# First two units of an RWKV-6 and SiLU kernel: values of the first queries in array quarters, a key turn moved behind the products for x, values reversed by VectorE

## Chip, cores and metric

The kernel runs on one core of one Trainium2 chip. The metric is the device time of one execution in microseconds (us). Three runs of the kernel before gave 600.97, 601.18 and 601.67 us, so its median is 601.18.

## What is computed

The reference is an attention block of the RWKV-6 kind (4 batches, 8 heads, 768 tokens, 48 channels a head), whose output becomes x of a two-layer block with a SiLU between the layers. All data are float32.

```python
for t in range(S):
    cur = np.einsum('bhd,bhe->bhde', u[None] * kt, vt)
    y[:, :, t] = np.einsum('bhd,bhde->bhe', rt, state + cur)
    state = wt[:, :, :, None] * state + np.einsum('bhd,bhe->bhde', kt, vt)
x = y.transpose(0, 2, 1, 3).reshape(3072, 384)
h = x @ w_in                                   # 384 x 2048
out = (h * (1.0 / (1.0 + np.exp(-h)))) @ w_out # 2048 x 384
```

## The kernel before

**Units.** The recurrence is cut into chunks of 128 tokens. A unit is one chunk of two batches (NB = 2, called b below); there are 12 units. Within a chunk the output is a masked product: scores of queries against keys, then scores times values, plus what the state of earlier chunks gives. Queries and keys of the heads lie in pairs: head 2p is on partitions 0 to 47 and head 2p + 1 on 64 to 111 (e = 0 and 1). Scores are built in seven levels (`scores(i, l)`): level l is the part of the triangle in which query and key are in sibling blocks of 2^l tokens. TensorE makes the products of a level into PSUM (L704, L712), and VectorE copies the part that the level's mask keeps into `score` (`keep_masked`, L722); some parts are copied by ScalarE (L741). Between levels the keys and queries are multiplied by products of w: `grow_keys` on GpSimd (L645), `grow_queries` on VectorE (L627), `odd_keys` on ScalarE (L615), `product` on GpSimd (L422), `start_keys` (L669), `odd_ones` (L659). The diagonal with u is a sum over channels (`bonus`, `bonus_sum`), spread by a small matmul (`bonus_spread`, L590) and written into `score` by VectorE (`bonus_write`, L604).

**The second batch stands in reverse.** For b = 1 keys, scores and values are kept with the tokens of the chunk in reverse order. In `score` the partition is the key. For the first 64 queries only the keys of the first 64 tokens count: partitions 0 to 63 for b = 0, and 64 to 127 for b = 1; the other half of those columns of `score` holds zeros. The values of b = 1 therefore have to be reversed as well: `reverse_v` (L410). In units 0 and 1 their load (`load_values`, L138) brings the 128 tokens in order, TensorE multiplies them by a mirrored identity (L414), and ScalarE copies the product back (L415). From unit 2 on the load comes in four DMAs of 32 tokens, the four groups in reverse order (L143), and one VectorE `stream_shuffle` reverses the 32 partitions within each group (L417).

**Outputs of a unit.** In units 0 and 1 there is no earlier state. `y(i, b)` (L873) makes scores times values: for each pair p and each e one matmul of 128 keys by 64 columns (48 channels and 16 that are overwritten or not used), over 128 queries (L879), into one PSUM bank per b; ScalarE copies it out to `yt` (L883). `dense_x(i, b)` then makes x from `yt` with twelve records of 128x128 matmuls (L917) and ScalarE, in one case VectorE, copies it into `xt` (L919). `turn_apart(i)` (L814) turns the grown keys back to token rows with 16 transposes (L820), `turn_k` copies them out (L828), and `update(i, b)` makes from them and the values the new state (L893; copied by L909). From unit 2 on, `y_state` and `y_values` do the work of `y`; they already take the first 64 queries of half of the heads with 64 keys alone (L851), and the rest with 128 keys (L865).

**The layers.** `up(i, m)` makes 256 hidden columns of a unit's 256 tokens (L1001), and ScalarE applies SiLU (L1010). `down` (L1023) and, later, `quarter` (L1067) make the output.

**Weights are rounded on the way.** In the first 100 us the 16 pieces of the weights are loaded (`load_weight`, L206) and each is rounded by a chain over three engines: ScalarE's `tail_weight` (L231, into the PSUM tile p_w) and `head_weight` (L223, L225), VectorE's `join_weight` (L242, L243, which first needs that ScalarE part and frees p_w at its end), GpSimd's `add_weight` (L255). A later piece is loaded into the place that a joined one has left. The diagonal of unit 0 also sits in p_w until L604 has read it.

**Order.** The order is written by hand: the steps stand in lists that `do` calls one after the other, and each engine takes its own instructions in that order. The first two units are written out step by step (L1108 to L1164), the others by `mix`. All loads in this part go through SP's queue, each issue also waiting for the landing of the issue eight places before it. The part around the change is, from the end of unit 0's scores:

```python
do((bonus, 1, 0), (bonus, 1, 1), (bonus, 1, 2), *both(y, 0), (turn_apart, 0), (join_weight, 0), (add_weight,),
   (product, 1, 0), (tail_weight, 1), (turn, 1, 0, "k"), (join_weight, 1), (dense_x, 0, 0), (turn, 1, 1, "k"),
   (dense_x, 0, 1), (grow_queries, 1, 0), (odd_ones, 1), (tail_weight, 2), (turn_k, 0), (head_weight, 2),
```

PSUM tiles p_m and p_sc are two banks each, taken by turns by `bank`; p_h has two buffers. `y(0, b)` uses p_h, `y(1, b)` uses p_m.

Of the kernel before, what the change touches and what calls it, by code (L numbers as in the profile page):

```python
# [8 lines left out]
F32 = mybir.dt.float32  # L9
# [29 lines left out]
def kernel(  # L39
# [11 lines left out]
    nc = tc.nc  # L51

    B, H, S, D = r.shape
    DM, DF = moe_w_in.shape
    L = 128
    NL = 7
    NB = 2
    NP = H // 2
    PD = 64
# [8 lines left out]
    NTOK = 2  # L68
# [8 lines left out]
    ps = ctx.enter_context(tc.tile_pool(name="ps", bufs=1, space=bass.MemoryType.PSUM))  # L77
# [6 lines left out]
    def bank(name, *dims):  # L84

        have = banks[name][turns_of[name] % 2][:]
        turns_of[name] += 1
        steps, n = [], 1
        for d in dims[::-1]:
            steps.insert(0, [n, d])  # L90
            n *= d
        return bass.AP(tensor=have.tensor, offset=have.offset, ap=[have.ap[0], *steps])
# [4 lines left out]
    vt, vq, whole = {}, {}, {}  # L97
# [28 lines left out]
    def load_values(i):  # L126
        n, b0 = units[i]
        t0 = n * L

        rooms = [pin.tile([128, H * D + PD - D], F32, name=name, bufs=2) for name in ("vt", "vq")]  # L130
        if n == 0:
            for room in rooms:
                nc.vector.memset(room[:, H * D:], 0.0)
        whole[i] = rooms
        vt[i], vq[i] = (room[:, 0:H * D].rearrange("p (h d) -> p h d", h=H) for room in rooms)
        nc.sync.dma_start(out=vt[i], in_=v[b0, :, t0:t0 + L, :].rearrange("h t d -> t h d"))
        if i < NTOK:
            nc.sync.dma_start(out=vq[i], in_=v[b0 + 1, :, t0:t0 + L, :].rearrange("h t d -> t h d"))  # L138
            return

        for g in range(4):
            t1 = t0 + L - (g + 1) * 32
            nc.sync.dma_start(out=vq[i][g * 32:(g + 1) * 32], in_=v[b0 + 1, :, t1:t1 + 32, :].rearrange("h t d -> t h d"))  # L143
# [134 lines left out]
    load_tokens(1)  # L278
    load_weight(1)
    load_values(0)  # L280
    for i in due[-1][2:]:
        load_weight(i)
    load_values(1)

    ident = const.tile([128, 128], F32, name="ident")
# [47 lines left out]
    NSC = 1  # L333
    score = const.tile([128, NSC, 2, Q, L], F32, name="score")
# [74 lines left out]

    def reverse_v(i):  # L410
        flat = vq[i].rearrange("p h d -> p (h d)")
        if i < NTOK:
            p_v = bank("p_m", H * D)
            nc.tensor.matmul(p_v, lhsT=mirror, rhs=flat, start=True, stop=True)  # L414
            nc.scalar.copy(out=flat, in_=p_v)  # L415
            return
        nc.vector.stream_shuffle(out=flat, in_=flat, mask=list(range(31, -1, -1)))  # L417
# [53 lines left out]
    at = 768  # L471
# [358 lines left out]
    p_yt, p_kv, yt = {}, {}, {}  # L830
# [28 lines left out]
    def y_values(i, e):  # L859
# [9 lines left out]
        for x in range(2):  # L869
            nc.scalar.copy(out=yt[i][PD * e:PD * e + D, x::2, :, :],  # L870
                           in_=p_yt[i, e][PD * x:PD * x + D].rearrange("p (q b) t -> p q b t", b=NB))

    def y(i, b):  # L873

        p_yt[i, b] = ps.tile([128, NP, L], F32, name="p_h", bufs=2) if i == 0 else bank("p_m", NP, L)
        for p in range(NP):
            for e in range(2):
                h = 2 * p + e
                nc.tensor.matmul(p_yt[i, b][PD * e:PD * e + PD, p, :], lhsT=whole[i][b][:, h * D:h * D + PD],  # L879
                                 rhs=score[:, i % NSC, e, b * NP + p, :], start=(p == 0), stop=(p == NP - 1))  # L880
        if b == 0:
            yt[i] = pt.tile([128, NP, NB, L], F32, name="yt", bufs=1)
        nc.scalar.copy(out=yt[i][:, :, b, :], in_=p_yt[i, b])  # L883
# [49 lines left out]
    def both(fn, i, *args):  # L933
        return [(fn, i, b, *args) for b in range(NB)]
# [159 lines left out]
    def do(*steps):  # L1094
        for fn, *args in steps:
            fn(*args)
# [20 lines left out]
    for l in range(1, NL):  # L1117
        do((scores, 0, l), *[(grow_keys, 0, l + 1)] * (l + 1 < NL), *others[l])

    do((bonus, 1, 0), (bonus, 1, 1), (bonus, 1, 2), *both(y, 0), (turn_apart, 0), (join_weight, 0), (add_weight,),  # L1120
       (product, 1, 0), (tail_weight, 1), (turn, 1, 0, "k"), (join_weight, 1), (dense_x, 0, 0), (turn, 1, 1, "k"),
       (dense_x, 0, 1), (grow_queries, 1, 0), (odd_ones, 1), (tail_weight, 2), (turn_k, 0), (head_weight, 2),
       (start_keys, 1, nc.gpsimd, True), (add_weight,), (up, 0, 0), (join_weight, 2), *blocks[4:8],
       (start_keys, 1, nc.gpsimd, False), (add_weight,), (tail_weight, 3), (odd_keys, 1, 1), (head_weight, 3), (grow_keys, 1, 1),
       (scores, 1, 1, (join_weight, 3)), (add_weight,), (up, 0, 1), (tail_weight, 4), (grow_keys, 1, 2), (head_weight, 4),
# [1 line left out]


    others = {1: [(bonus_sum, 1, 0), (bonus_sum, 1, 1), (load_rk, 2), *blocks[8:12]], 2: [*both(update, 0)],
              3: [(bonus_spread, 1), (reverse_v, 1), (clear, 1), (load_values, 2)]}  # L1130

    def piece(i):

# [2 lines left out]
    for m in range(1, 4):  # L1136
        do((piece, m + 3), (scores, 1, m + 1), (grow_keys, 1, m + 2), (up, 0, m + 2), *others[m])
    do((head_weight, 8), (join_weight, 7), (scores, 1, 5), (grow_keys, 1, 6), (add_weight,), (tail_weight, 8), (up, 0, 6),
       (bonus_write, 1))

    do((scores, 1, NL - 1), (bonus, 2, 0), (bonus, 2, 1), (join_weight, 8), (add_weight,), (bonus_sum, 2, 0), (bonus, 2, 2), (up, 0, 7), *both(y, 1), (turn_apart, 1),
       (tail_weight, 9), (turn_k, 1), (dense_x, 1, 0), (head_weight, 9, [0]), (dense_x, 1, 1), (head_weight, 9, [1]),
       (join_weight, 9), (add_weight,), (tail_weight, 10), (head_weight, 10), *both(update, 1), (bonus_sum, 2, 1), (load_rk, 3), (up, 1, 0), *both(turn, 2, "w"))
    blocks = block_loads(3)
# [64 lines left out]
```

## Time and profile before

| | us |
|---|---|
| median of three runs | 601.18 |
| the profiled execution | 601.21 |
| its span in the profile | 599.4 |
| TensorE busy (matmuls) | 591.4 |
| VectorE busy | 415.2 |
| GpSimd busy | 363.6 |
| ScalarE busy | 232.8 |

Times in the profile count from the start of the span. PE is TensorE, PEld its weight loads, DVE VectorE, ACT ScalarE, POOL GpSimd and SP the queue that issues loads. A float32 matmul is recorded as two records, so "x32" on L879 is 16 matmuls. A busy TensorE isn't TensorE at its peak, since matmuls overlap and their ends are modelled. Instructions of ScalarE, VectorE and GpSimd overlap their neighbours by up to about 0.1 us, so starts are the better measure. The granted clock of TensorE is 1.0 over the whole span.

The stretches that the change touches: unit 0's y at 29.4 to 32, its x at 32.5 to 36, unit 1's `reverse_v` at 58.8 to 60.3, unit 1's y at 66.7 to 68.6, and its x at 69.2 to 72.2. Busy times there, from the table of windows:

| window | PE | DVE | ACT | POOL |
|---|---|---|---|---|
| 26 to 36 | 9.37 | 8.17 | 6.89 | 8.59 |
| 36 to 46 | 9.24 | 7.90 | 9.69 | 10.00 |
| 46 to 56 | 9.49 | 9.69 | 9.01 | 7.89 |
| 56 to 64 | 7.91 | 7.73 | 7.18 | 7.55 |
| 64 to 76 | 12.00 | 8.82 | 9.69 | 8.17 |
| 76 to 90 | 13.60 | 11.53 | 11.70 | 10.97 |

### The profile page before, as it was taken

To read this page: it belongs to the slowest core of one execution; us is meant where nothing else is said; L and a number is where in the kernel's file an instruction comes from. 1 tells how busy PE (TensorE), PEld (TensorE's weight loads), DVE (VectorE), ACT (ScalarE), POOL (GpSimd) and SP (SyncE) were. 2 spreads that over 40 slices of the span, in tenths; PEclk is the share of its full clock that TensorE was granted. 3 is DMA by queue.
4 is the path that set the end of the run, shared out by engine and by line. 5 is a ranking of instruction groups with operands and counts; after the bars stand their busy time and mean duration, and the time that the engine had idled before them with its cause. 6 is when DMAs were issued, how large, how long until landed. Compare 5 with 4: busy or idle time off the path is not lost.

```text
span 599.4 us, 15477 instructions
## 1 busy us (share of the span) xinstructions
PE 591.4 (99%) x6142; PEld 529.8 (88%) x6142; DVE 415.2 (69%) x709; ACT 232.8 (39%) x516; POOL 363.6 (61%) x414
## 2 busy tenths in 40 slices
PE   8999999999999999999999999999999999999997
PEld 8787876799899899899889889889889889889997
DVE  7879788798696695696695696686587587551041
ACT  6788884431530530540440351361351242240110
POOL 6998778357678668278478478478478558500000
PEclk9999999999999999999999999999999999999999
DMA  9966793343542543642642643643553531101000
GB/s 227 299 145 165 161 298 47 58 77 48 128 61 59 108 65 56 136 61 52 137 61 52 137 65 54 131 61 53 118 76 53 115 55 27 37 2 27 27 1 26
DMA packets 203080, 53.45 MB, mean 89 GB/s; under 512 B 186752, under 2 KB 194816, under 8 KB 203008
## 3 DMA queue, kind: packets, MB, share of 16 engines
q1 hardware_dynamic: 201424, 51.88, 42.1%
q8 instruction: 48, 0.79, 0.5%
q10 hardware_dynamic: 1584, 0.59, 0.5%
q14 instruction: 24, 0.20, 0.1%
HBM read 43.21 MB, written 5.24 MB: 81 GB/s over the span
## 4 chain that ended last, share of the span: by engine, by line
PE 87%; POOL 5%; DVE 4%; ACT 3%; issue 1%; POOLq 0%; DVEq 0%; ACTq 0%
PE p_h L1001 38%; PE p_o L1067 33%; PE p_m L1023 3%; PE p_sc L704 3%; PE p_m L865 2%; PE p_m L844 2%; PE p_m L704 2%; POOL w_in_sb L255 1%; POOL tk L645 1%; PE p_sc L893 1%; POOL w_out_sb L255 1%; DVE score L722 1%; PE p_m L820 1%; POOL tw L422 1%; DVE p_w L242 1%
## 5 line engine op out<-in xcount | busy, mean ns | idle before, releaser
L1001 PE MATMUL p_h<-xt,w_in_sb 128*128 128x256 f32 x1152 | 258.9, 382 | 0.8 <-POOL tk L669 0.7
L1001 PEld LDWEIGHTS p_h<-xt,w_in_sb 128*128 128x128 f32 x1152 | 215.9, 190 | 31.8 <-POOL tk L669 0.9
L1010 ACT ACTIVATE gt<-p_h 128x512 f32<-128x512 f32 x90 | 53.5, 596 | 181.5 <-PE p_h L1001 181.2
L645 POOL TENSOR_TENSOR tk<-tk,tw 128x256 f32<-128x256 f32 x128 | 94.5, 760 | 35.1 <-issue 21.0
L1067 PE MATMUL p_o<-own,temps 128*128 128x192 f32 x528 | 88.1, 326 | 0.1
L1067 PE MATMUL p_o<-w_out_sb,gt 128*128 128x192 f32 x508 | 87.4, 328 | 0.0
L1067 PEld LDWEIGHTS p_o<-own,temps 128*128 128x128 f32 x528 | 86.0, 190 | 0.5 <-DVE temps L1076 0.4
L507 POOL TENSOR_TENSOR ruk<-tokens_rk 128x768 f32<-128x768 f32 (+1 forms) x32 | 51.0, 1606 | 55.8 <-DMA tokens_rk<-in_k_dram 40.2
L1067 PEld LDWEIGHTS p_o<-w_out_sb,gt 128*128 128x128 f32 x508 | 82.7, 190 | 0.6
L1049 DVE TENSOR_TENSOR temps<-gt 128x256 f32<-128x256 f32 x84 | 57.8, 688 | 22.4 <-ACT gt L1010 22.4
L422 POOL TENSOR_TENSOR tw<-tw 128x256 f32<-128x256 f32 (+6 forms) x83 | 43.5, 524 | 35.8 <-DVE tw L374 31.9
L627 DVE TENSOR_TENSOR tr<-tr,tw 128x512 f32<-128x512 f32 x61 | 52.6, 862 | 18.0 <-PE p_m L704 14.3
L615 ACT COPY tk<-tk 128x256 f32<-128x256 f32 x52 | 21.0, 403 | 101.6 <-POOL tk L645 68.2
L722 DVE COPY_PREDICATED score<-mask,p_sc 128x512 f32<-128x512 int8 x42 | 31.2, 798 | 3.5 <-PE p_sc L704 3.3
L1049 DVE TENSOR_TENSOR temps<-temps,gt 128x256 f32<-128x256 f32 x43 | 32.3, 752 | 1.5
L1076 DVE TENSOR_TENSOR temps<-p_o,partial 128x192 f32<-128x192 f32 x22 | 7.9, 357 | 34.0 <-PE p_o L1067 24.8
L1076 DVE TENSOR_TENSOR partial<-p_o,partial 128x192 f32<-128x192 f32 x33 | 11.7, 356 | 28.2 <-PE p_o L1067 28.2
L1067 PE MATMUL p_o<-w_out_sb,temps 128*128 128x192 f32 x176 | 30.4, 326 | 0.0
L870 ACT COPY yt<-p_m 48x512 f32<-48x512 f32 x40 | 23.2, 580 | 15.7 <-PE p_m L865 11.9
L541 DVE TENSOR_REDUCE block_sums<-ruk 128x4 f32<-128x192 f32 (+1 forms) x48 | 24.2, 546 | 7.1 <-POOL ruk L507 7.1
L1067 PEld LDWEIGHTS p_o<-w_out_sb,temps 128*128 128x128 f32 x176 | 28.9, 190 | 0.0
L898 POOL TENSOR_TENSOR state<-state,tw 128x512 f32<-128x512 f32 x16 | 21.9, 1386 | 10.3 <-PE p_m L844 10.3
(191 smaller groups left out, 816.8 us busy)
## 6 DMA issues: line engine op xcount, KB each, us to landing
w_out_sb<-in_moe_w_in_dram SPq DMA_DIRECT2D x6, 768.0 KB, 7.7
w_out_sb<-in_moe_w_out_dram SPq DMA_DIRECT2D x4, 768.0 KB, 5.7
own<-in_moe_w_out_dram SPq DMA_DIRECT2D x4, 768.0 KB, 6.0
tokens_rk<-in_r_dram SPq DMA_DIRECT2D x8, 384.0 KB, 4.3
tokens_rk<-in_k_dram SPq DMA_DIRECT2D x8, 384.0 KB, 5.3
tokens_w<-in_w_dram SPq DMA_DIRECT2D x8, 384.0 KB, 6.5
xt<-yt SPq DMA_DIRECT2D x60, 48.0 KB, 1.9
raw<-in_w_dram SPq DMA_DIRECT2D x80, 32.0 KB, 2.0
```

The lines of the kernel that those rows point to most:

```text
L422: engine.tensor_tensor(out=up, in0=t[:, :, 0::2], in1=t[:, :, 1::2], op=ALU.mult)
L507: mul = lambda out, one, two: nc.gpsimd.tensor_tensor(out=out, in0=one, in1=two, op=ALU.mult)
L541: add = lambda out, have: nc.vector.tensor_reduce(out=out, in_=have, axis=mybir.AxisListType.X, op=ALU.add)
L627: nc.vector.tensor_tensor(out=odd, in0=odd, in1=tw[i][l][:, :, 0::2][:, :, :, None].to_broadcast([128, Q, L >> (l + 1), c]), op=ALU.mult)
L645: nc.gpsimd.tensor_tensor(out=out, in0=have, in1=odd_products(i, l, b, *blocks), op=ALU.mult)
L704: nc.tensor.matmul(to, lhsT=tk[i][rows, X[l % 2] + p, x * m:(x + 1) * m], rhs=have, start=True, stop=True)
L722: nc.vector.copy_predicated(out=dst, mask=masks[l][:, :, None].to_broadcast([128, NB, NP, ni, c]), data=sc[e].rearrange("p (b q) (i c) -> ...
L870: nc.scalar.copy(out=yt[i][PD * e:PD * e + D, x::2, :, :], in_=p_yt[i, e][PD * x:PD * x + D].rearrange("p (q b) t -> p q b t", b=NB))
L1001: nc.tensor.matmul(p_h[:, a, :], lhsT=w_in_sb[:, c, f * 128:(f + 1) * 128], rhs=xt[i][:, c, :], start=(c == 0), stop=(c == KC - 1))
L1010: nc.scalar.activation(out=gt[i, m], in_=p_h, func=AF.Silu)
L1049: nc.vector.tensor_tensor(out=out, in0=one, in1=two, op=op)
L1067: nc.tensor.matmul(p, lhsT=left(f), rhs=right[:, f, :], start=(f == 0), stop=(f == FH - 1))
```

## The change

It has three parts, all in units 0 and 1.

- y in quarters: a new step `y_first(i)` takes the first 64 queries of all heads and both b. For each p, e and b it is one matmul of 64 keys (the half that counts) by 64 columns over 64 queries, so that e and b together address the four quarters of the array, into the two banks of the two b. It starts the accumulation. `y(i, b)` then takes only the last 64 queries, with all 128 keys.
- `turn_apart(0)` moves from between y and `dense_x(0, 0)` to behind `dense_x(0, 1)`. `turn_k(0)` stays where it is in ScalarE's order.
- `reverse_v(1)` takes the form of the later units: four loads of 32 tokens in reverse order of the groups, and VectorE's shuffle in place of TensorE's product and ScalarE's copy. It stands later: behind `scores(1, 5)` and `up(0, 6)`, right ahead of `bonus_write(1)`. Unit 0 keeps its form.

```diff
-        if i < NTOK:
+        if i == 0:
             nc.sync.dma_start(out=vq[i], in_=v[b0 + 1, :, t0:t0 + L, :].rearrange("h t d -> t h d"))
             return
...
     def reverse_v(i):
         flat = vq[i].rearrange("p h d -> p (h d)")
-        if i < NTOK:
+        if i == 0:
             p_v = bank("p_m", H * D)
...
+    def y_first(i):
+
+        half = L // 2
+        for b in range(NB):
+            p_yt[i, b] = ps.tile([128, NP, L], F32, name="p_h", bufs=2) if i == 0 else bank("p_m", NP, L)
+        for p in range(NP):
+            for e in range(2):
+                for b in range(NB):
+                    at, rows = (2 * p + e) * D, slice(b * half, (b + 1) * half)
+                    nc.tensor.matmul(p_yt[i, b][PD * e:PD * e + PD, p, 0:half], lhsT=whole[i][b][rows, at:at + PD],
+                                     rhs=score[rows, i % NSC, e, b * NP + p, 0:half], start=(p == 0), stop=False)
+
     def y(i, b):
 
-        p_yt[i, b] = ps.tile([128, NP, L], F32, name="p_h", bufs=2) if i == 0 else bank("p_m", NP, L)
+        half = L // 2
         for p in range(NP):
             for e in range(2):
                 h = 2 * p + e
-                nc.tensor.matmul(p_yt[i, b][PD * e:PD * e + PD, p, :], lhsT=whole[i][b][:, h * D:h * D + PD],
-                                 rhs=score[:, i % NSC, e, b * NP + p, :], start=(p == 0), stop=(p == NP - 1))
+                nc.tensor.matmul(p_yt[i, b][PD * e:PD * e + PD, p, half:], lhsT=whole[i][b][:, h * D:h * D + PD],
+                                 rhs=score[:, i % NSC, e, b * NP + p, half:], start=False, stop=(p == NP - 1))
...
-    do((bonus, 1, 0), (bonus, 1, 1), (bonus, 1, 2), *both(y, 0), (turn_apart, 0), (join_weight, 0), (add_weight,),
+    do((bonus, 1, 0), (bonus, 1, 1), (bonus, 1, 2), (y_first, 0), *both(y, 0), (join_weight, 0), (add_weight,),
...
-       (dense_x, 0, 1), (grow_queries, 1, 0), (odd_ones, 1), (tail_weight, 2), (turn_k, 0), (head_weight, 2),
+       (dense_x, 0, 1), (turn_apart, 0), (grow_queries, 1, 0), (odd_ones, 1), (tail_weight, 2), (turn_k, 0), (head_weight, 2),
...
-              3: [(bonus_spread, 1), (reverse_v, 1), (clear, 1), (load_values, 2)]}
+              3: [(bonus_spread, 1), (clear, 1), (load_values, 2)]}
...
-       (bonus_write, 1))
+       (reverse_v, 1), (bonus_write, 1))
...
-    do((scores, 1, NL - 1), (bonus, 2, 0), (bonus, 2, 1), (join_weight, 8), (add_weight,), (bonus_sum, 2, 0), (bonus, 2, 2), (up, 0, 7), *both(y, 1), (turn_apart, 1),
+    do((scores, 1, NL - 1), (bonus, 2, 0), (bonus, 2, 1), (join_weight, 8), (add_weight,), (bonus_sum, 2, 0), (bonus, 2, 2), (up, 0, 7), (y_first, 1), *both(y, 1), (turn_apart, 1),
```

## The prediction

> **What bounds the kernel now.** I read the page's chain of work first, as it says which stretches can pass a saving on to the end.
>
> ```profile
> PE 87%; POOL 5%; DVE 4%; ACT 3%; issue 1%; POOLq 0%; DVEq 0%; ACTq 0%
> ```
>
> Then the same chain asked for the first 92 us alone, since all three edits lie there (pieces: start, us, what).
>
> ```profile
> 39.83 0.78 ACT p_w L231
> ...
> 40.63 0.97 DVE p_w L242
> ...
> 56.76 1.83 POOL w_in_sb L255
> ...
> 63.92 2.86 PE p_h L1001 x12
> 66.77 1.90 PE p_m L879 x32
> 68.67 0.63 PE p_sc L820 x16
> 69.30 2.89 PE p_m L917 x24
> ...
> 89.15 0.70 PE p_sc L704 x32
> ```
>
> From 89.15 on TensorE is nearly solid (40.00 of 40.00 us busy from 90 to 130, 466.05 of 469.00 after it), and its one later stall, 0.44 us at 132.56, hangs on a VectorE run that an event on TensorE at 114 starts. So the whole remainder moves with 89.15. Before it the path is mostly the rounding of the weights: ScalarE, VectorE and GpSimd in turn, with TensorE on it only from 63.92 to 72.2. Third, the timeline around each edit (start, us, engine, line, what; idle before it and who ended that). Unit 0's y:
>
> ```profile
> 31.12 0.58 ACT L883 COPY yt<-p_h 128x512 f32<-128x512 f32 x1 [1.10 <-PE p_h L879]
> ...
> 31.99 0.59 ACT L883 COPY yt<-p_h 128x512 f32<-128x512 f32 x1 [0.29 <-PE p_h L879]
> ...
> 34.16 0.48 ACT L919 COPY xt<-p_h 128x384 f32<-128x384 f32 x1 [0.19 <-PE p_h L917]
> ...
> 40.63 0.96 DVE L242 SCALAR_TENSOR_TENSOR p_w<-w_out_sb,p_w 128x768 uint32<-128x768 uint32 x1 [1.87 <-ACT p_w L231]
> ```
>
> ScalarE waits twice for TensorE (0.29, 0.19), then runs without a break to the L231 that starts at 39.73 (the chain picks it up at 39.83), and VectorE sits idle 1.87 us for that. From 40.63 VectorE is busy almost without a gap to 67.84. Unit 1's y and what follows:
>
> ```profile
> 66.70 0.85 PEld L879 LDWEIGHTS p_m<-score,vt 128*64 128x64 f32 x16 [0.33 <-issue]
> ...
> 73.14 1.12 DVE L909 COPY state<-p_m 48x384 f32<-48x384 f32 x2 [1.07 <-PE p_m L893]
> ...
> 88.38 0.92 ACT L223 ACTIVATE temps<-own 128x768 bf16<-128x768 bf16 x1 [0.98 <-DMA own<-in_moe_w_out_dram]
> ```
>
> y(1) starts when up(0,7) ends, 0.78 us after VectorE is done with the scores (its last L722 runs 65.19 to 65.92). TensorE's update at 72.10 releases L909, after which VectorE runs to L243 (77.55 to 78.50), which releases the GpSimd chain at 78.64. The last line is the one place where a load is late.
>
> **What the Trainium skill says.** "TensorEngine Tiling (Array Packing)", Key Properties: a change of tiling mode drains the array. Agrees: weight loads stand idle 0.33 us ahead of L879 at 66.70 with nothing waited for, 0.17 us ahead of L820, about 0.17 between L851 and L865. Same page, Instruction Overhead: about 60 cycles per matmul, so 64 columns still pay. Agrees: for column pairs the pitch falls from 52 ns at 128 columns (15 further L879 loads in 0.77 us) to 26 at 64 (L865: 8 in 0.21). "VectorE: DVE Perf Modes", the tier table: STREAM_SHUFFLE has the 1x mode only; the trace has the duration, 578 to 586 ns (L417). "Perfetto Trace Analysis", DMA Instruction (HWDGE): a DMA issue's profiled window holds waiting for the generator and making descriptors. Agrees: the issue of one 192 KB load takes 0.41 us at 71.58 and 5.69 at 22.00 (L138), when the DMA engines are full.
>
> **Part A, y in quarters.** Sixteen 128x64 matmuls of 128 columns go; sixteen 64x64 ones of 64 columns (four quadrants) and sixteen 128x64 ones of 64 columns come, each two records. Old: 66.70 to 68.60, 1.90 us, with the drain behind. New: a quadrant block of 32 records with its drain is L704's, 54.72 to 55.33, 0.61 us; then 32 records at 26 to 28 ns, 0.86; then 0.17 drain: 1.64. Saving 0.25; I take **0.2** (bounds 0 and 0.35: L851's 18 ns per record instead of 14 costs 0.15, no extra drain gives 0.1). At unit 1 this is on TensorE's path 66.7 to 72.1 and goes through the update and L909 to 78.64, so it counts in full. The first half y(1,0) ends 0.2 later, but turn_apart stands between it and dense_x. At unit 0 the first yt copy comes 0.2 later (about 31.32) and the second can follow it without its 0.29 wait (31.83).
>
> **Part B, turn_apart(0) behind dense_x(0).** Nothing is added; 16 transposes (0.63 us with drain) move. dense_x(0,0) then starts at the end of the first yt copy, about 31.95 and not 32.51, so ScalarE's xt copy no longer waits: second yt copy 31.83, L231 32.31, two tk copies, xt copy at 33.71 in place of 34.16. The ScalarE run shifts by 0.45. Next late: up(0,0). It needs the second xt copy, which VectorE does after L243 (ends 35.35, earlier by 0.16 to 0.2), so it starts 0.23 earlier and ends at 38.80; SiLU L1010 then starts at 38.84 in place of 39.26. turn_apart ends about 35.45, ahead of that copy's end (35.83), so it is hidden behind it; without that cover it would cost 0.63. kq's copies come at 36.2, after it. So L231 and VectorE's L242 come **0.4** earlier (bounds 0.2 and 0.5). Does 0.4 last from 40.2 to 63.9? VectorE is the late one throughout: the L231s it needs later have 0.65 us or more in hand, GpSimd idles 1.52 us at 52.98 and 0.23 at 56.72 for VectorE, ScalarE 0.77 at 52.87. Then GpSimd's L255 at 56.72 and 62.04 and up(0,7) at 63.92 all come 0.4 earlier.
>
> **Part C, reverse_v(1).** Off TensorE: 2 records at 58.84, 0.89 us, but scores(1,5) next waited 0.55 for GpSimd's L645, so nothing is gained. Off ScalarE: 0.48 and 0.61 of waiting, at 59.2 to 60.3; ScalarE idles 1.44 before 66.81, so nothing. On VectorE: 0.59 us in front of L604, behind which are L604, the last L722 (then y(1)) and L242/L243. L722 ends at 66.51 less 0.4; up(0,7) ends at 66.70 less 0.4: it fits with 0.2 us to spare, cost nothing. Were VectorE not 0.78 ahead it would cost 0.59. GpSimd's L255 at 68.31 waits for that L243, and has 1.7 us idle later. The p_m banks change parity from here; each use follows the same predecessor by turns, cost nothing.
>
> Its loads: SP issues four DMAs where it issued one, ahead of unit 2's w, k, r blocks and of every later weight. A steady issue costs 0.48 us (five L123 in 2.42), so SP falls behind by d, at most 3 x 0.49 = 1.5; below nothing is excluded, as the bytes are the same. The one issue was held up 5.69 us by full engines, and splitting it mostly splits that wait: I take d = 0.3. SP has no idle to recover d, so the load at 82.75 lands d later than 88.35; from L223 on ScalarE, VectorE (idle 1.74 at 91.11) and GpSimd follow to L645, which ends at 105.29. TensorE needs that for the burst at 106.37, or 105.74 after a gain of 0.63. So d up to 0.45 is free, each us above costs one.
>
> **Sum.** 0.4 (B with A at unit 0) + 0.2 (A at unit 1) + 0 (C) = 0.6 us. The profiled execution took 601.21 (span 599.4 and 1.8 around it), 0.03 over the median 601.18; 601.2 - 0.6 = **600.6**. What a measurement of this kernel can tell from no change is about 0.2%, 1.2 us, so I forecast no difference by that bound.
>
> **The rivals.**
> (1) SP decides: d = 1.5. The loads at 88.35 and 90.80 come 1.5 later, L645 ends at 106.79, TensorE's burst at about 106.85 instead of 106.37: 0.5 slower than before, 601.7. For: SP issues back to back from 28 to 71. Against: the 5.69 us. It decides from d = 1.1, where the whole gain is gone. Slower, by less than can be measured.
> (2) The gain is swallowed: SiLU at 39.26 stays put by up(0,0), or GpSimd (busy all 10.00 us of 36 to 46) holds VectorE, and the extra drain eats A. 601.2. For: GpSimd is solid from 32.08 and doesn't move. Against: VectorE's calculated starts are all later than what GpSimd gives.
> (3) Quarters cost less and yt's waits vanish wholly: 0.5 + 0.35 = 0.85, with ScalarE's freed 1.1 us at 59 helping the rounding: up to 1.1, so 600.1 to 600.4; take 600.3. Against: VectorE holds that stretch.
>
> **Chances.** Forecast 0.50 (own span 600.3 to 600.9), (1) 0.15, (2) 0.22, (3) 0.13. Past 1.2 us either way I see no single mechanism; I leave 0.08 for faster (the top of 3) and 0.07 for slower (1 with a load that TensorE meets twice). Same: 0.85. Range 600.1 to 601.7: from (3) to (1).
>
> **What would show it.** In the profile after: the xt copy follows its tk copies with no wait near 33.7; VectorE's L242 near 40.2; up(0,7) near 63.5; the y block of unit 1 about 1.65 us to turn_apart; L604 0.6 later against L722, with y still starting at up(0,7)'s end; TensorE's L704 at 88.5 in place of 89.15. Wrong: if up(0,0) doesn't move, if y(1) waits for VectorE, or if SP's L206 at 82.75 comes over 0.5 later and TensorE idles near 106.

## The result, and the profile after

The changed kernel took 603.08 us in the median of nine runs (602.77 to 604.23), beside 601.67 of the kernel before on the same chip (600.97 to 601.92): a ratio of 1.003 with a 95% interval of 1.0021 to 1.0039. It is 1.4 us slower, where 0.6 us faster was forecast. The profiled execution took 603.59, its span 601.8. Line numbers behind the new step are 12 higher: y is L882 (quarters) and L891 (last 64 queries), yt's copy L895, dense_x L929 and L931, up L1013, SiLU L1022.

The chain of work of the kernel after, by engine; transfers (DMA) and SP have come into it:

```profile
PE 88%; POOL 3%; DMA 3%; DVE 2%; ACT 1%; issue 1%; SPq 1%; POOLq 0%; ACTq 0%; DVEq 0%
```

The timeline of the kernel after around unit 0's y and x (start, us, engine, line, what; idle before it and who ended that):

```profile
31.78 1.07 ACT L895 COPY yt<-p_h 128x512 f32<-128x512 f32 x2 [0.95 <-PE p_h L891]
...
36.11 0.41 ACT L394 COPY tk<-p_m 128x256 f32<-128x256 f32 x1 [2.38 <-PE p_sc L820]
...
36.66 0.49 ACT L931 COPY xt<-p_h 128x384 f32<-128x384 f32 x1
...
39.25 0.96 DVE L242 SCALAR_TENSOR_TENSOR p_w<-w_out_sb,p_w 128x768 uint32<-128x768 uint32 x1 [2.47 <-ACT p_w L231]
```

yt's two copies now follow each other, as forecast. But ScalarE's L394, which had no wait before, now waits 2.38 us for L820, the moved transposes. L394 writes unit 1's keys into `tk`, and `tk` has one buffer: it can't be written before turn_apart(0) has read unit 0's keys out of it (B alone, below, tests this). Behind L394 in ScalarE's order stand the copy of xt (36.66, before 34.16) and L231 (38.33, before 35.80), and VectorE waits for that.

The chain of the kernel after over the first 92 us (start, us, what):

```profile
35.36 0.65 PE p_sc L820 x16
...
36.11 0.41 ACT tk L394
...
66.31 2.86 PE p_h L1013 x12
69.16 0.63 PE p_m L882 x32
69.79 1.08 PE p_m L891 x32
70.87 0.63 PE p_sc L820 x13
...
91.38 0.62 PE p_sc L704 x26
```

The last up of unit 0 starts 2.39 us later than before, L704 2.23 later, and the span is 2.4 longer. 0.80 of that is there at 28.93 us (GpSimd's L452), ahead of the change. That start differs from execution to execution: over the twenty traces of this case it lies between 0.36 us earlier and 0.80 later than in the kernel before, with the change or without it. y(1) takes 1.71 us (69.16 to 70.87) where it took 1.90. C shows as forecast: the shuffle L417 takes 0.61 us at 64.40, VectorE is done with the scores at 68.24, and y(1) starts at up(0,7)'s end.

### The profile page after: what moved, and what is told of

The parts are those of the page before. It is cut to its first block, busy times and chain, and to the rows that moved or that the text cites. A ratio compares the mean times of both kernels' runs of the same rounds, so it can differ in the third digit from the quotient of the medians.

```text
span 601.8 us, 15601 instructions
## 1 busy us (share of the span) xinstructions
PE 589.9 (98%) x6204; PEld 528.6 (88%) x6204; DVE 413.1 (69%) x711; ACT 232.4 (39%) x515; POOL 366.1 (61%) x414
## 4 chain that ended last, share of the span: by engine, by line
PE 88%; POOL 3%; DMA 3%; DVE 2%; ACT 1%; issue 1%; SPq 1%; POOLq 0%; ACTq 0%; DVEq 0%
PE p_h L1013 38%; PE p_o L1079 33%; PE p_m L1035 3%; PE p_sc L704 3%; PE p_m L865 2%; PE p_m L844 2%; PE p_m L704 2%; DMA w_out_sb<-in_moe_w_out_dram 1%; DMA raw<-in_r_dram 1%; PE p_m L386 1%; PE p_sc L905 1%; POOL w_out_sb L255 1%; PE p_m L820 1%; POOL tk L645 1%; POOL w_in_sb L255 1%
## 5 line engine op out<-in xcount | busy, mean ns | idle before, releaser
L1013 PE MATMUL p_h<-xt,w_in_sb 128*128 128x256 f32 x1152 | 259.2, 382 | 2.4 <-ACT xt L931 1.3
L1013 PEld LDWEIGHTS p_h<-xt,w_in_sb 128*128 128x128 f32 x1152 | 215.8, 190 | 33.7 <-POOL w_in_sb L255 1.7
L1022 ACT ACTIVATE gt<-p_h 128x512 f32<-128x512 f32 x90 | 53.5, 596 | 184.8 <-PE p_h L1013 184.5
L645 POOL TENSOR_TENSOR tk<-tk,tw 128x256 f32<-128x256 f32 x128 | 94.5, 759 | 35.7 <-issue 22.1
L507 POOL TENSOR_TENSOR ruk<-tokens_rk 128x768 f32<-128x768 f32 (+1 forms) x32 | 53.0, 1668 | 51.7 <-DMA tokens_rk<-in_k_dram 32.0
L627 DVE TENSOR_TENSOR tr<-tr,tw 128x512 f32<-128x512 f32 x61 | 54.4, 892 | 19.3 <-PE p_m L704 15.8
L1061 DVE TENSOR_TENSOR temps<-temps,gt 128x256 f32<-128x256 f32 x43 | 30.6, 710 | 1.5
L704 PEld LDWEIGHTS p_sc<-tr,tk 48*32 48x32 f32 (+1 forms) x1312 | 18.3, 119 | 11.3 <-issue 6.9
```

The lines of the kernel that those rows point to most:

```text
L507: mul = lambda out, one, two: nc.gpsimd.tensor_tensor(out=out, in0=one, in1=two, op=ALU.mult)
L627: nc.vector.tensor_tensor(out=odd, in0=odd, in1=tw[i][l][:, :, 0::2][:, :, :, None].to_broadcast([128, Q, L >> (l + 1), c]), op=ALU.mult)
L645: nc.gpsimd.tensor_tensor(out=out, in0=have, in1=odd_products(i, l, b, *blocks), op=ALU.mult)
L704: nc.tensor.matmul(to, lhsT=tk[i][rows, X[l % 2] + p, x * m:(x + 1) * m], rhs=have, start=True, stop=True)
L1013: nc.tensor.matmul(p_h[:, a, :], lhsT=w_in_sb[:, c, f * 128:(f + 1) * 128], rhs=xt[i][:, c, :], start=(c == 0), stop=(c == KC - 1))
L1022: nc.scalar.activation(out=gt[i, m], in_=p_h, func=AF.Silu)
```

## Experiments

Each kernel was timed in five rounds beside the kernel before on the same chip. "Ratio" is to the kernel before, with its 95% interval. Line numbers differ from kernel to kernel; where the text names a step without a line shown, it goes by those of before.

The expectations name four theories. T1: the moved transposes hold up the write of `tk`. T2: the quarters cost time by themselves. T3: C's three more loads make later loads land later. T4: A's lead meets loads that can't come sooner. "Quarters" is part A.

| kernel | median us | before | ratio |
|---|---|---|---|
| A and C, B undone | 602.88 | 601.77 | 1.0013 (1.0002 to 1.0024) |
| B alone | 603.13 | 601.77 | 1.0021 (1.0014 to 1.0029) |
| all, keys in a place of their own | 602.39 | 601.77 | 1.0008 (0.9994 to 1.0022) |
| all, transposes between the halves | 603.13 | 601.77 | 1.0022 (1.0011 to 1.0034) |
| A alone | 602.17 | 601.72 | 1.0012 (1.0000 to 1.0023) |
| C alone | 601.90 | 601.72 | 0.9999 (0.9991 to 1.0007) |
| C's four loads alone | 602.01 | 601.72 | 1.0001 (0.9992 to 1.0010) |
| A and B, own place | 602.53 | 601.72 | 1.0012 (1.0001 to 1.0023) |
| A alone again | 603.34 | 601.70 | 1.0020 (1.0005 to 1.0036) |
| A, padded | 602.86 | 601.70 | 1.0019 (1.0008 to 1.0030) |
| A, small DMAs on ScalarE | 603.99 | 601.70 | 1.0045 (1.0028 to 1.0061) |
| before, the same | 603.47 | 601.70 | 1.0029 (1.0018 to 1.0040) |
| A, value loads later | 604.52 | 601.80 | 1.0036 (1.0024 to 1.0049) |
| before, the same | 602.55 | 601.80 | 1.0022 (1.0009 to 1.0035) |
| A in unit 1 only | 601.96 | 601.80 | 1.0001 (0.9987 to 1.0015) |
| all, own place, value loads later | 605.78 | 601.80 | 1.0064 (1.0041 to 1.0087) |
| A, r and k of unit 3 later | 603.51 | 601.62 | 1.0025 (1.0014 to 1.0036) |
| before, the same | 601.57 | 601.62 | 0.9994 (0.9984 to 1.0004) |

Single runs of one kernel lie up to 5 us apart: A alone from 600.87 to 605.40, ten of its 22 above 603. The kernel before, beside it, has the same ends (600.91 to 605.28), but only eight of 67 above 603. B alone lies between 602.70 and 604.33: its lowest run is 1.8 us above the lowest of before (600.90). Five kernels can't be told from before, as their intervals hold 1: all with the keys in their own place, C alone, its four loads alone, A in unit 1 only, and before with r and k later; that of A alone begins at 1. At the fast end the quarters do show a gain: the lowest runs of A again, all with own place, and A and B with own place are 600.73, 600.71 and 600.57, where those of before beside them are 600.92, 600.90 and 600.91.

**B, alone and undone.**

```diff
-    ... *both(y, 0), (turn_apart, 0), (join_weight, 0), ...
+    ... *both(y, 0), (join_weight, 0), ...
-       (dense_x, 0, 1), (grow_queries, 1, 0), ...
+       (dense_x, 0, 1), (turn_apart, 0), (grow_queries, 1, 0), ...
```

> The kernel before with turn_apart(0) alone moved behind dense_x(0, 1). T1: slower than before by 1.3 to 1.9 us; L394 waits for L820 some 2 us, the first L242 behind it comes 1.3 to 1.9 later. T2 and T3: no difference within 0.3 us.

The timeline of B alone:

```profile
35.23 0.39 ACT L394 COPY tk<-p_m 128x256 f32<-128x256 f32 x1 [2.22 <-PE p_sc L820]
...
35.78 0.49 ACT L919 COPY xt<-p_h 128x384 f32<-128x384 f32 x1
...
38.35 0.96 DVE L242 SCALAR_TENSOR_TENSOR p_w<-w_out_sb,p_w 128x768 uint32<-128x768 uint32 x1 [2.28 <-ACT p_w L231]
```

With nothing else changed L394 waits 2.22 us for the transposes, and GpSimd at 50.57 is 1.78 us later against its own L452. So B by itself costs what the whole change costs (1.4 us in the median).

Then the reverse, the whole change with that one step put back:

```diff
-    ... (y_first, 0), *both(y, 0), (join_weight, 0), ...
+    ... (y_first, 0), *both(y, 0), (turn_apart, 0), (join_weight, 0), ...
-       (dense_x, 0, 1), (turn_apart, 0), (grow_queries, 1, 0), ...
+       (dense_x, 0, 1), (grow_queries, 1, 0), ...
```

> Quarters for both y and the new reverse_v(1), with turn_apart(0) back between y and dense_x(0, 0). T1 (the moved transposes are the last readers of unit 0's keys, and ScalarE's L394, which writes unit 1's keys into the same buffer, waits for them ahead of the copy of xt): the wait of L394 is gone, and what is left is y's 0.2 us and up to 0.2 from ScalarE, so 0.2 to 0.4 us faster than before, some 1.6 to 2.0 faster than the whole change. T2 (the quarters cost time): 1.0 to 1.4 slower than before. T3 (the four loads of values, or a later start of the loads, cost it): also 1.0 to 1.4 slower than before.

L394's wait is gone (33.51, none), but the kernel is still 1.1 us slower than before. T1 was expected to leave a gain; it left a second cost.

**The same change without the wait.** Unit 0's keys get a place that nobody else uses until 47 us:

```diff
+            if (i, name) == (0, "k"):
+                t = rooms[:, 4 * 2 * PW - rows * L:].bitcast(F32).rearrange("p (q t) -> p q t", q=rows)
+            else:
+                t = pt.tile([128, rows, L], F32, name="t" + name, bufs=2 if name == "r" else 1)
```

> The whole change, but unit 0's keys lie in a place of their own (a third of own and the spare buffer, free until 47 us), so that nothing that writes unit 1's keys waits for turn_apart(0). T1: L394 doesn't wait for L820, the xt copy stands near 33.7, and the whole is 0.4 to 0.7 us faster than before, as the prediction had it. T2 and T3: as the whole change, 1.0 to 1.4 slower than before. A third theory, that the move costs for another reason (up(0, 0), VectorE's copy of xt): slower than before although L394's wait is gone.

The timeline of this kernel (its lines are 5 higher):

```profile
33.48 0.40 ACT L399 COPY tk<-p_m 128x256 f32<-128x256 f32 x1
...
34.03 0.49 ACT L936 COPY xt<-p_h 128x384 f32<-128x384 f32 x1
```

ScalarE runs through without waiting, and in this execution the lead that the prediction wanted is there: GpSimd at 50.57 is 0.48 us early against its own start. That settles the wait's cause: nothing changed but the place of the keys. The time, though, is not below before: 0.6 us above it in the median, which can't be told from it.

A smaller dose of the same wait:

```diff
-       ... (dense_x, 0, 0), (turn, 1, 1, "k"),
-       (dense_x, 0, 1), (turn_apart, 0), (grow_queries, 1, 0), ...
+       ... (dense_x, 0, 0), (turn_apart, 0), (turn, 1, 1, "k"),
+       (dense_x, 0, 1), (grow_queries, 1, 0), ...
```

> The whole change, with turn_apart(0) between dense_x(0, 0) and dense_x(0, 1): the transposes end some 1.4 us earlier than in the whole change, so that L394 waits about 0.5 and not about 2 us against its time in the kernel before. T1: L394's wait shrinks with that, and the time is within 0.3 us of before, so 1.2 to 1.7 faster than the whole change. T2 and T3: as the whole change, 1.0 to 1.4 slower than before.

The transposes end at 33.61, and L394 follows at 33.73, 1.03 us after ScalarE was free (the view names GpSimd's L255, which ends at 33.70 by chance; in the kernel before L394 starts while that L255 runs). By 50.57 the stretch stands 0.17 us behind before, so the dose answers as T1 says: a shorter hold, a smaller loss. The total doesn't: 603.13. Something later adds to it.

**The other two parts, one by one.** A alone and C alone are the lines of the diff above that belong to them, put into the kernel before.

> The kernel before with the first queries' values in quarters in both units, nothing else. After the first four runs, T3 (the three more loads of C make the later loads of weights land later, which TensorE meets at 90 to 107 us) expects 0.2 to 0.4 us faster than before. T2 (the quarters cost time by themselves) expects what quarters and new values together showed, 0.8 to 1.2 us slower than before.

A is 0.45 us slower in the median (602.17 to 601.72), just at the edge of what can be told from before.

> The kernel before with the new form of reverse_v(1) alone: four loads, VectorE's shuffle. T3: 0.8 to 1.4 us slower than before, with the weight loads that are issued near 75 us landing about 1.2 us later than in the kernel before and the load after them issued 1.2 us later. T2: no difference within 0.3 us.

601.90 to 601.72: no difference.

```diff
-            t1 = t0 + L - (g + 1) * 32
+            t1 = t0 + (g * 32 if i < NTOK else L - (g + 1) * 32)
```

> The kernel before, with unit 1's values of the second batch loaded in four DMAs of 32 tokens in their given order, TensorE's product and ScalarE's copy as before: only the three more loads of C. T3: as C alone, 0.8 to 1.4 us slower than before. If it is C's place or engine that costs (VectorE's 0.6 us), no difference within 0.3 us.

602.01: none either. (The load takes C's four-DMA form too, with the groups in their given order.) The next kernel is the one with keys in their own place, less C.

> The change without C, and with a place of their own for unit 0's keys: A and B without the wait of L394. T3 with T1: what the prediction forecast, 0.4 to 0.7 us faster than before, and 0.8 to 1.4 faster than the same with C. T2: 0.4 to 0.8 slower than before.

602.53, 0.8 above before: the forecast gain isn't there without C. T3 falls: C and its loads can't be told from before. What is left is A. And yet T2 ("the quarters cost by themselves") doesn't fit the traces. The table gives, for a GpSimd instruction at three places and for the end of the span, how much later it comes than in the kernel before, less the same difference at L452 (28.93 us); below zero is a lead. The last column adds up ScalarE's waits for weight loads at its six L223 between 73 and 95 us. Each row is one execution. That of before (601.21) lies some 0.5 us below its medians here, so an end of 0.5 is no loss; those of A with small DMAs on ScalarE, with value loads later, and with r and k later are the slowest of their kernels (607.01, 606.65, 604.96).

| kernel | 50.57 (L645) | 73.60 (L255) | 107.23 (L645) | end | waits |
|---|---|---|---|---|---|
| before | 0 | 0 | 0 | 0 | 0.98 |
| B alone | 1.78 | 1.78 | 1.80 | 2.21 | 0 |
| the whole change | 1.50 | 1.39 | 1.42 | 1.59 | 0.86 |
| all, between the halves | 0.17 | 0.06 | 1.45 | 2.07 | 3.22 |
| C alone | 0.02 | 0.10 | -0.05 | 0.62 | 1.14 |
| C's four loads alone | 0.01 | 0.02 | -0.13 | 0.78 | 1.30 |
| before, r and k of unit 3 later | 0.00 | 0.00 | 0.00 | 0.32 | 0 |
| before, small DMAs on ScalarE | 0.00 | 0.00 | 0.00 | 1.57 | 0 |
| before, value loads later | -0.01 | -0.02 | 0.77 | 0.81 | 2.31 |
| A alone | -0.48 | -0.63 | -0.28 | 1.13 | 2.78 |
| A alone again | -0.45 | -0.65 | 0.50 | 0.87 | 3.39 |
| A and B, own place | -0.51 | -0.69 | 0.60 | 0.99 | 3.76 |
| all, own place | -0.48 | -0.58 | -0.44 | 0.13 | 2.00 |
| A and C | -0.51 | -0.62 | -0.03 | 1.42 | 2.73 |
| A, padded | -0.46 | -0.44 | -0.40 | -0.40 | 0.33 |
| A in unit 1 only | 0.00 | -0.18 | 1.26 | 1.29 | 3.76 |
| A, r and k of unit 3 later | -0.47 | -0.38 | 0.95 | 3.91 | 4.74 |
| A, small DMAs on ScalarE | -0.49 | -0.68 | 2.85 | 5.21 | 4.42 |
| A, value loads later | -0.01 | -0.18 | 4.59 | 5.32 | 4.80 |
| all, own place, value loads later | -0.49 | -0.57 | 3.82 | 4.93 | 4.02 |

A alone leads by 0.45 to 0.48 at 50 us and by 0.63 to 0.65 at 73 us. That is the whole forecast gain, and B without its wait adds 0.03 to it. The chain of A alone shows why:

```profile
31.73 1.84 POOL w_in_sb L255
...
45.32 1.27 POOL tk L645 x2
46.59 0.03 issue
46.62 0.86 DVE tr L627
```

From 31.73 to 46.59 GpSimd is the late one. An xt copy that comes sooner doesn't shorten that.

**Where A's lead goes.** Between 73 and 107 us the kernels with quarters fall back, by 0.03 to 1.44 us with the loads in their old order (3.53 in the run with small DMAs on ScalarE); in those without quarters it moves by 0.15 at most. ScalarE's timeline of A again, at the weights:

```profile
80.76 0.95 ACT L223 ACTIVATE temps<-w_out_sb 128x768 bf16<-128x768 bf16 x1 [0.86 <-DMA w_out_sb<-in_moe_w_out_dram]
...
84.43 0.93 ACT L223 ACTIVATE temps<-w_out_sb 128x768 bf16<-128x768 bf16 x1 [0.26 <-DMA w_out_sb<-in_moe_w_out_dram]
...
90.03 0.92 ACT L223 ACTIVATE temps<-own 128x768 bf16<-128x768 bf16 x1 [2.27 <-DMA own<-in_moe_w_out_dram]
```

and of the kernel before, the first of them:

```profile
79.94 0.95 ACT L223 ACTIVATE temps<-w_out_sb 128x768 bf16<-128x768 bf16 x1
```

That load landed at 79.92 in the kernel before, 0.02 us ahead of its reader: there was no room for a lead. And the one read at 88.38 was 0.98 us late for its reader already, though off the path. That is T4: the loads set the pace from 75 us on. The next runs test it.

> The quarters alone once more, for a second profile and beside the next three on the same chip. T4 (A does free 0.5 to 0.6 us up to 90 us, but TensorE then meets DMAs that SP can't issue sooner, and waits about 1 us now and then between 90 and 300 us) and T2 (the quarters themselves cost) both expect 0.2 to 0.8 us slower than before in the median. In the profile T4 expects GpSimd at 73 us some 0.6 us earlier against the start of unit 0's key growth than before, and the loss at later waits for a DMA; T2 expects no lead at 73 us.

```diff
-    ... (up, 0, 7), (y_first, 1), *both(y, 1), ...
+    ... (up, 0, 7), (beat, 1), (beat, 1), (y_first, 1), *both(y, 1), ...
```

> The quarters alone, and two idle transposes (about 0.46 us of TensorE) ahead of unit 1's y, which lie on the path: they take back most of A's lead. T2: their 0.46 us come on top, so about 0.9 us slower than before. T4: with the lead gone TensorE meets the DMAs as in the kernel before: within 0.3 us of before, and not slower than the quarters without them.

The lead at 73 us came again in A alone, 0.65. Padding (two idle transposes ahead of y(1)) took only 0.2 of it, not most, and doesn't bring before's time back: 602.86 is 1.16 above before, where T4 said within 0.3. A miss for T4. It doesn't show T2's sum either, as 602.86 and the 603.34 of A beside it can't be told apart. The padded kernel's profiled run (601.26, its second lowest) shows something else. In it the weight load read at 88.38 came early enough, and A's lead, 0.40, is kept to the end:

```profile
87.75 0.92 ACT L223 ACTIVATE temps<-own 128x768 bf16<-128x768 bf16 x1 [0.33 <-DMA own<-in_moe_w_out_dram]
```

So a lead is not lost of necessity: it is lost in the executions in which the loads are late.

```diff
-                nc.sync.dma_start(out=diag[i][b][s::2], in_=own_sums[...])
+                (nc.scalar if i == 3 else nc.sync).dma_start(out=diag[i][b][s::2], in_=own_sums[...])
```

> The quarters alone, with unit 3's four small DMAs diag<-own_sums issued on ScalarE's queue and not behind the block loads on SP's. In the quarters' first profile ScalarE waited 2.73 us for one of them at 155.35, with the copies that release TensorE queued behind it (TensorE idle 0.96 us at 157.86). T4: that wait is gone, the time is 0.3 to 0.8 us less than that of the quarters alone, so between 0.3 faster than before and equal to it. T2: as the quarters alone.

> The kernel before with the same four DMAs on ScalarE's queue, as the control. T4: no more than 0.3 us faster than before, as TensorE has no wait at that place in the kernel before. If it gains as much as the quarters do, the wait is not a matter of A's lead.

The reason for this pair is a later place of the same kind. The timeline of A alone:

```profile
155.35 0.20 ACT L595 COPY both_b<-diag 128x16 f32<-128x16 f32 x1 [2.73 <-DMA diag<-own_sums]
...
157.86 4.37 PE L1013 MATMUL p_h<-xt,w_in_sb 128*128 128x256 f32 x19 [0.96 <-ACT gt L1022]
```

ScalarE waits for a small DMA that stands behind SP's block loads, SiLU stands behind ScalarE, and TensorE idles 0.96 us. The edit was no remedy: ScalarE issues the four DMAs in order, from 152.40 to 154.87, its SiLU stands behind them, and TensorE then idles 1.27 us in the kernel before too. The edit costs 1.8 us in the control, so the pair decides nothing about A. (In the profiled run of A with this edit most of the loss, 3.53, is there by 107 us, ahead of the edit.)

The value loads of unit 2, moved on SP's queue in three kernels:

```diff
-              3: [(bonus_spread, 1), (reverse_v, 1), (clear, 1), (load_values, 2)]}
+              3: [(bonus_spread, 1), (reverse_v, 1), (clear, 1)]}
-    do((scores, 1, NL - 1), ..., (join_weight, 8), (add_weight,), ...
+    do((scores, 1, NL - 1), ..., (join_weight, 8), (load_values, 2), (add_weight,), ...
```

> The quarters alone, with unit 2's five value loads moved on SP's queue behind the weight load that follows them (issued near 75 us until now). T4 (the loads of weights 12 to 14, not TensorE, set the pace from 75 to 107 us, and A's lead meets them): that load lands some 3 us earlier, L223 no longer starts at a landing, and the lead of 0.6 us is kept, so 0.3 to 0.8 us faster than before, and 0.8 to 2.0 faster than the quarters alone. T2 (the quarters themselves cost): as the quarters alone, 0.5 to 1.6 slower than before.

> The kernel before with the same move of the five loads. T4: within 0.3 us of before, or a little faster, since its TensorE and VectorE have no lead that a load could take; fewer slow runs. T2 says nothing of it. If it gains as much as the quarters with the move do, the quarters' own gain isn't there.

> The whole change, with a place of their own for unit 0's keys and the five value loads behind the weight load: both obstacles that the theory names are gone. T1 with T4: 0.3 to 0.8 us faster than before, 1.7 to 2.2 faster than the change. T2: 0.5 to 1.2 slower than before.

A miss in the direction. The timeline of A with the value loads later:

```profile
92.17 0.90 ACT L223 ACTIVATE temps<-own 128x768 bf16<-128x768 bf16 x1 [4.80 <-DMA own<-in_moe_w_out_dram]
...
100.77 0.69 PE L704 MATMUL p_sc<-tr,tk 48*64 48x64 f32 x32 [2.49 <-POOL tk L645]
```

The value loads, now between two weight loads, took up to 2.52 us each to issue (0.41 to 1.29 before). The weight load that landed at 88.35 in the kernel before landed at 92.15, and TensorE idled 2.49 us. (This trace had no lead at 50 us, so it loses more than a lead.) Without quarters the same edit costs 0.75 us in the median; in its trace that load landed at 89.74, and the stretch was 0.77 late at 107 us. In the whole change it costs 4.0 (TensorE idle 2.61 us at 99.73). So these loads do set the pace, with quarters and without; the order tried was a worse one.

Unit 0 with y in its old form:

```diff
-       ... (bonus, 1, 2), (y_first, 0), *both(y, 0), ...
+       ... (bonus, 1, 2), *both(y, 0), ...
     def y(i, b):
-        half = L // 2
+        half = L // 2 if i > 0 else 0
```

> The quarters in unit 1 only, y of unit 0 as before. The lead at 73 us is then 0.2 and not 0.65 us. T4: the loads are met by less, within 0.3 us of before (0.3 to 1.3 less than the quarters in both units). T2 (the quarters cost): half of what both cost, 0.2 to 0.8 slower than before.

No difference from before in the median, as T4 says. Its profiled run (602.31) is above its median and loses 1.44 us up to 107 us all the same, with a lead of 0.18 only, so this speaks for T4 only by the times.

Last, one weight load ahead of the loads of r and k for unit 3:

```diff
-       ... (bonus_sum, 2, 1), (load_rk, 3), (up, 1, 0), *both(turn, 2, "w"))
+       ... (bonus_sum, 2, 1), (up, 1, 0), *both(turn, 2, "w"))
-    others = {0: [(up, 1, 1), ...
+    others = {0: [(load_rk, 3), (up, 1, 1), ...
```

> The quarters alone, with the four loads of r and k for unit 3 (read from 142 us on) moved on SP's queue behind the weight load that was issued behind them at 82 to 85 us. T4: that weight load is issued near 79 us and lands by 86 us, L223 no longer waits for it at 88 us, A's lead of 0.6 us at 73 us passes 107 us, and the time is 0.3 to 0.8 us less than before, 0.8 to 2.4 less than the quarters alone; slow runs are rarer. T2 (the quarters cost): 0.5 to 1.6 slower than before.

> The kernel before with the same move of the four loads. T4: without a lead little is gained, 0 to 0.4 us faster than before, and its slow runs are rarer; the quarters add 0.3 to 0.6 us to that. If both are equal, the quarters gain nothing even when the load is in time.

The load was issued earlier in both (80.86 and 78.67 instead of 82.75). In the control it came in time (L223 at 87.38 instead of 88.38), and the control gained nothing (0.00 at 107 us): in the kernel before, that wait isn't on the path. A stayed at 1.0025. In its profiled run the load still held up L223 by 0.58 us, two others did more (2.17 us at 77.98, 1.71 at 93.48), and then the small DMA (TensorE idle 1.35 us at 159.76). So moving this one load is no remedy; whether A would gain with all its loads in time isn't shown.

Nor is 107 us the last place. A alone is still 0.27 early at 148 us and loses 1.41 at the small DMA of 155 us. C alone, which has no lead, loses 0.49 there, so that place isn't A's own. A and C has a lead of 0.02 left at 199 us and loses 1.27 at another small DMA of SP's queue, for which TensorE itself waits:

```profile
240.79 3.48 PE L1013 MATMUL p_h<-xt,w_in_sb 128*128 128x256 f32 x15 [1.04 <-DMA xt<-yt]
```

**What makes the loads later.** A lead that meets a load would be lost, not turned into a loss. So A must also delay loads. The DMA view of 71 to 80 us, of the kernel before (queue: packets, MB, share; then loads, KB, median us to landing):

```profile
q1 hardware_dynamic: 3078, 2.39, 90.4%
...
w_out_sb<-in_moe_w_out_dram SPq DMA_DIRECT2D x2, 768.0 KB, 5.7
```

and of A again:

```profile
q1 hardware_dynamic: 3556, 2.14, 88.6%
q8 instruction: 1, 0.02, 0.8%
...
w_out_sb<-in_moe_w_out_dram SPq DMA_DIRECT2D x2, 768.0 KB, 6.7
```

An instruction load of 16 KB (queue q8) falls on the value and weight loads. The issue that it meets on SP is long; SP's timeline, of before and of A again:

```profile
75.05 0.90 SPq L206 DMA_DIRECT2D w_out_sb<-in_moe_w_out_dram  x2
...
82.75 1.07 SPq L206 DMA_DIRECT2D own<-in_moe_w_out_dram  x2
```

```profile
75.61 1.95 SPq L206 DMA_DIRECT2D w_out_sb<-in_moe_w_out_dram  x2
...
85.13 1.07 SPq L206 DMA_DIRECT2D own<-in_moe_w_out_dram  x2
```

The queue passes such a delay on. An issue waits for the landing eight places before it, and eight places behind the second of these weight loads stands the last load of k for unit 3, right ahead of the next weight load. In all fifteen traces with this order the next weight load is issued 0.72 or 0.73 us after that landing: at 82.75 after 82.03 in the kernel before, at 85.13 after 84.41 in A again. So 2.38 us of a late landing are 2.38 us of a late issue of the load that L223 waits for at 88.38.

Over the whole span the kernels without quarters have 48 instruction loads, those with quarters 49. They fit TensorE's instructions by their number: 6142 matmul and as many weight load records, at the 64 bytes an instruction that the Trainium skill gives ("Trainium Architecture — The Big Picture", The software stack), are an estimated 786 KB, 48.0 loads of 16 KB; quarters add 64 of each, 8 KB, and make it 48.5. In before and in the other kernels that have neither quarters nor B these loads lie near 70 and 90 us (less the difference of starts); with quarters in both units they lie at 67 to 70 and at 73 to 77. In eleven of twelve such traces one SP issue in that stretch took 1.17 to 2.52 us (1.04 in the twelfth; full engines make such issues too: 1.29 at 73.65 in the kernel before), and where it was the second weight load at 75 to 76 us (four traces) that load took 7.8 to 8.7 us to land instead of 6.5. With quarters in unit 1 only it lies at 82.6 us.

This fits times and traces, but no run moved an instruction load alone, and there is evidence against it as the whole cause. Two traces with one at 75 us (A padded, all with own place) lost almost nothing up to 107 us. Four with quarters (A and B with own place, unit 1 only, small DMAs on ScalarE, r and k later) were late before it came: the weight load that SP issues at 71.09 in the kernel before was 1.3 to 1.9 us later there, less the difference of starts. And that issue lies anywhere between 69.43 and 73.33 us over the twenty traces, so that one trace of a kernel can't tell the kernel's delay from the execution's. So: that the lead, where it was followed here, is lost to waits for DMAs of SP's queue is shown; that the moved instruction load is what turns it into a cost is argued, and stays open.

## Why the prediction was wrong, point by point

- **Part A, unit 0.** Right: the second copy of yt follows the first without the 0.29 wait, and the stretch is 0.45 to 0.51 early at 50 us in nine of the ten traces with quarters in both units and the transposes out of the way (the tenth, value loads later, is level). The sum gave 0.4 to "B with A"; A alone brings it.
- **Part A, unit 1.** Right: 1.71 instead of 1.90, 0.19 for 0.2. The lead grows by 0.15 to 0.20 up to 73 us without C and by 0.08 to 0.11 with it (padding and r and k later apart).
- **Part B.** This is the step that failed: "Nothing is added; 16 transposes move". It priced where the transposes go and what they hide behind (the second xt copy), and took up(0,0) as the one that waits next. It counted the "two tk copies" among ScalarE's steps as free to run, and didn't ask who still reads what they overwrite. L394 came 2.0 (whole change) to 2.3 us later (B alone), 1.8 us of it on the path (B alone). With A's lead of 0.5 against it, 2.0 makes the 1.5 us by which the whole change is late at 50 us, and that stays to its end (1.59). And with that wait taken away B was worth 0.03 and not its share of 0.4, for the reason that rival (2) gave: GpSimd is solid from 31.7 to 46.6 us in the chain of A alone.
- **Part C.** Right, both that it is free and that SP has taken up the three more DMAs by 55 us (55.18 in both traces); C alone is 0.9999 (0.10 late at 73 us in its trace, no longer at 107).
- **The carry to the end.** "So the whole remainder moves with 89.15" failed for A. The prediction saw the load that is late at 88.38, and its "d up to 0.45 is free" counts the gain in. But d stood for C's loads alone: that with A the loads could land later was put at nothing without a reason, and the load with 0.02 us in hand at 79.92 wasn't priced. In A alone and A again L223 at 88.38 came 0.29 and 1.04 us later than before, less the difference of starts, and a gain of 0.6 us became 0.45 to 1.6 us of cost (medians of the two timings).
- **The rivals.** (1) named the place (loads from 82 us, TensorE at 105), but with C as the cause; it is not what slowed the whole change. None had a wait on the buffer of the keys. "Past 1.2 us either way I see no single mechanism" was wrong by that one.
- **The parts don't add.** B alone costs 1.4 us in the median and A 0.5 to 1.6, the whole change 1.4. In its trace the stretch is 1.4 us late at 73 us and loses nothing to the loads up to 107 us (1.39 to 1.42). A kernel that is late anyway has time for its loads.

No kernel tried beats the kernel before in the median; the five named under the first table can't be told from it.

## What to carry to other kernels

When a step moves, list the tiles that it reads, and for each the next write into the same buffer: that write now waits for the moved step, and everything behind it in its engine's order waits with it. Before a saving is credited to the end, look ahead for the first load whose reader starts within a few hundredths of its landing; where that load is late, the saving stops there. And small matmuls may have a price beside their time, which was not shown apart here: each is more instructions to load through the same DMA engines as the data.

## What the runs showed of the hardware

- Instructions arrive during the execution as packets of 16 KB on a DMA queue of their own, 48 or 49 in these kernels, nine in ten of them 0.9 to 1.5 us long. An SP issue that meets one near 75 us took 1.0 to 2.5 us, where others of its kind take 0.4 to 0.6.
- On a queue whose issues wait for the landing eight places before, a load that lands 2.38 us late makes a later one be issued 2.38 us late (84.41 and 85.13 us for 82.03 and 82.75).
- After TensorE had idled 2.49 us, its granted clock fell. The table of windows of A with the value loads later (us, TensorE busy, clock, DMA share, GB/s):

```profile
95.00:100.00 5.00, 3.01 (x13) 1.00 0.37 46
100.00:105.00 5.00, 4.23 (x39) 0.69 0.35 41
```

It was 0.50 from 101.90 to 105.30. The same came after idles of 2.21 us (0.74 in 90 to 95, A with the small DMAs on ScalarE) and 2.61 us (0.66 in 100 to 105, all with value loads later), and not after 1.84 us (A in unit 1 only, 1.00). The Trainium skill ("TensorE: Matmul & The Clock Gate", What's actually happening) halves the clock after an idle window of about 3.4 us; here less was enough. It adds to the cost of those three; no other profiled run shows it.
